# A transformer block of one core: order of every engine written by hand, attention in slices, opening tile by tile

## The chip, the cores and the metric

The kernel runs on one core of a Trainium2 chip. The metric is the time of one execution on the device in microseconds (us). "Span" is the time from the first to the last instruction of the one execution that was profiled; it is about 1.8 us shorter than the time that the same execution is given (842.8 against 844.55 us before). A run counts as slow when it takes over 1.5% more than the fastest run of its kernel; all timed runs below were in the fast state. The one exception is a single look whose state is not known, and it is named as such. In the views of the profile PE is TensorE, PEld its weight loads, DVE VectorE, ACT ScalarE, POOL GpSimd and SP SyncE; L12 is line 12 of that kernel's code.

## The reference, cut to what matters

One block: layernorm, a QKV projection, a sliding dilated attention (each position looks at 8 keys, two positions apart), an output projection with residual, a second layernorm, and a feed-forward part in which a gate product and an up product are multiplied and projected down.

```python
def _A_ref(x, wqkv, wo):                       # x: 1 x 2048 x 1024, 32 heads of 32
    q, k, v = split_heads(x @ wqkv)
    idx = pos[:, None] - 2 * arange(8)[None, :]          # 8 keys, dilation 2
    logits = einsum("bhsd,bhswd->bhsw", q, k[idx]) * scale      # masked where idx < 0
    o = einsum("bhsw,bhswd->bhsd", softmax(logits), v[idx])
    return merge_heads(o) @ wo
# ... (cut)
h  = x + _A_ref(layernorm(x), wqkv, wo)
n  = layernorm(h)
h2 = h + ((n @ w_gate) * (n @ w_up)) @ w_down            # 1024 -> 3584 -> 1024
```

## The kernel before

The 2048 positions are done in four chunks of 512. The matmuls run on TensorE and write to tiles in PSUM; such a tile can be filled anew when another engine has read it (`PE ps <- ACT sg` in the views below is a wait for that). The attention of a chunk has no matmul: VectorE does it as products, sums and a softmax over tiles of 128 partitions (4 parts of the chunk x 32 heads), which takes about 84 us a chunk. It needs a layout other than the one that the projections give, so ScalarE copies each QKV result out of PSUM, SyncE stores it to DRAM (`qd`, `kd`, `vd`), and GpSimd loads it back in the attention's layout (`qD`, `kD`, `vD`). The keys and values of a part include a halo, the positions just before it, which its first queries look at. The attention's result `oD` goes to DRAM and comes back transposed as `oT`, the operand of the output projection.

The order of instructions is left to the framework's scheduler, steered by priorities (`prio`); a low priority makes attention fill the gaps of everything else. Projections and feed-forward use six PSUM tiles, transposes two more.

```python
    psmm = ctx.enter_context(tc.tile_pool(name="psmm", bufs=6, space=PSUM))
    pstp = ctx.enter_context(tc.tile_pool(name="pstp", bufs=2, space=PSUM))
# ... (cut)
    def attention(c):
        qD = att.tile([128, DH, SUB], BF, tag="qD")
        kD = att.tile([128, DH, SUB + HB], BF, tag="kD")
        vD = att.tile([128, DH, SUB + HB], BF, tag="vD")
        nc.gpsimd.dma_start(qD[:], qd[c].rearrange("c g d s -> (c g) d s"))
        # ... (cut: halo copies DRAM to DRAM, loads of kD and vD, all on GpSimd)
        for wp in range(W // 2):
            prod = att.tile([128, 2, DH, SUB], BF, tag="prod")
            for j in range(2):
                o = HB - DIL * (2 * wp + j)
                nc.vector.tensor_tensor(prod[:, j], qD[:], kD[:, :, o:o + SUB], ALU.mult)
            # ... (cut: sums over DH, softmax, products with vD, sums into oD)
        nc.gpsimd.dma_start(od[c].rearrange("c g d s -> (c g) d s"), oD[:])
        for cp in range(4):
            nc.gpsimd.dma_start(oT[:, :, cp, :], od[c][cp].rearrange("(hg hl) d s -> (hl d) hg s", hl=4))
        return oT

    def wo_ln2(c, oT):
        # ... (cut: loads of four x tiles into hs, of the weights)
        for hf in range(2):
            for t in range(4):
                ps = psmm.tile([128, 512], F32, tag="mm")
                # ... (cut: 8 matmuls of oT and wo)
                nc.vector.tensor_tensor(hs[t][:, bass.ts(hf, 512)], ps[:], hs[t][:, bass.ts(hf, 512)], ALU.add)
        for t in range(4):
            layernorm_T(hs[t], lnT, t * 128)
        return lnT, hs
# ... (cut)
    for c in range(NCH):
        qkv(c, lnTs[c], B0)                       # blocks 0 to 2 of 6
        if c + 1 < NCH:
            with prio(-10000 + 1000 * (c + 1)):
                lnTs[c + 1] = ln1(c + 1)
        else:
            with prio(1000000):
                oT = attention(0)
            nxt = wo_ln2(0, oT)                   # between the halves of the last QKV
        qkv(c, lnTs[c], B1)
    for c in range(NCH):
        lnT2, hs = nxt
        hT = ffn1(c, lnT2)                        # gate/up
        if c + 1 < NCH:
            with prio(1000000 + (c + 1) * 20000):
                oT = attention(c + 1)
            nxt = wo_ln2(c + 1, oT)
        ffn2(c, hT, hs)                           # down
```

Of the kernel before, what the change touches and what calls it, by code (L numbers as in the profile page):

```python
# [16 lines left out]
D = 1024  # L17
H = 32
DH = 32
# [3 lines left out]
HALO = (W - 1) * DIL  # L23
# [7 lines left out]
NEG = -1.0e9  # L31




@with_exitstack
def kernel(
# [18 lines left out]
    @contextmanager  # L56
    def prio(base):
        with tc.high_priority(offset=tc.cur_priority - base):
            yield

    const = ctx.enter_context(tc.tile_pool(name="const", bufs=1))
    wpool = ctx.enter_context(tc.tile_pool(name="wstream", bufs=6))
    lnTp = ctx.enter_context(tc.tile_pool(name="lnT", bufs=3))
    lnp = ctx.enter_context(tc.tile_pool(name="ln", bufs=4))
    xp = ctx.enter_context(tc.tile_pool(name="xp", bufs=4))
# [4 lines left out]
    psmm = ctx.enter_context(tc.tile_pool(name="psmm", bufs=6, space=PSUM))  # L70
    pstp = ctx.enter_context(tc.tile_pool(name="pstp", bufs=2, space=PSUM))
    dram = ctx.enter_context(tc.tile_pool(name="dram", bufs=1, space=DRAM))

    nc.scalar.preload_act_table_set("natural_log_exp_and_others")
    ident = const.tile([128, 128], BF)
    make_identity(nc, ident[:])
    eps = const.tile([128, 1], F32)
    nc.vector.memset(eps[:], EPS)
    mask = const.tile([32, W, 16], F32)
    nc.vector.memset(mask[:], 0.0)  # L80
    for w in range(1, W):
        nc.vector.memset(mask[:, w, 0:DIL * w], NEG)
    zt = const.tile([32, DH, HB], BF)
    nc.vector.memset(zt[:], 0.0)
# [12 lines left out]
    def layernorm_T(src, dstT, col, xbar=True):  # L97
        st = small.tile([128, 2, nc.vector.BN_STATS_DIM], F32, tag="st")
        for i in range(2):
            nc.vector.bn_stats(out=st[:, i, :], in_=src[:, bass.ts(i, 512)])  # L100
        mv = small.tile([128, nc.vector.BN_AGGR_DIM], F32, tag="mv")
        nc.vector.bn_aggr(out=mv[:], in_=st[:])  # L102
        lnv = small.tile([128, 1], F32, tag="lnv")
        nc.scalar.activation(lnv[:], mv[:, 1:2], ACTF.Ln, bias=eps[:])  # L104
        rstd = small.tile([128, 1], F32, tag="rstd")
        nc.scalar.activation(rstd[:], lnv[:], ACTF.Exp, scale=-0.5)
        ln = lnp.tile([128, D], BF, tag="ln")
        nc.vector.tensor_scalar(ln[:], src[:], mv[:, 0:1], rstd[:], ALU.subtract, ALU.mult)
        if xbar:
            nc.sync.dma_start_transpose(dstT[:, :, col:col + 128], ln[:])  # L110
            return
        pt = pstp.tile([128, KO, 128], BF, tag="pt")
        for kk in range(KO):
            nc.tensor.transpose(pt[:, kk, :], ln[:, bass.ts(kk, 128)], ident[:])
        nc.scalar.copy(dstT[:, :, col:col + 128], pt[:])

    def ln1(c):
        lnT = lnTp.tile([128, KO, TC], BF, tag="lnT")
        for t in range(4):
            xt = xp.tile([128, D], BF, tag="x")  # L120
            nc.sync.dma_start(xt[:], x[bass.ds(c * TC + t * 128, 128), :])
            layernorm_T(xt, lnT, t * 128, xbar=(c > 0))
        return lnT

    wq_sb = []

    def qkv(c, lnT, blocks):
        for b in blocks:
            wt = wq_sb[b]
            pss = {}  # L130
            if c == 0 and b == 0:
                for j in range(4):
                    pss[j] = psmm.tile([128, TC], F32, tag="mm", name=f"ps0_{j}")
                for hf in range(2):
                    for j in range(4):
                        for ko in range(KO):
                            nc.tensor.matmul(pss[j][:, bass.ts(hf, 256)], lhsT=wt[:, ko, bass.ts(j, 128)],
                                             rhs=lnT[:, ko, bass.ts(hf, 256)],
                                             start=(ko == 0), stop=(ko == KO - 1))
            for j in range(4):  # L140
                m = b * 4 + j
                if j in pss:
                    ps = pss[j]
                else:
                    ps = psmm.tile([128, TC], F32, tag="mm")
                    for ko in range(KO):
                        nc.tensor.matmul(ps[:], lhsT=wt[:, ko, bass.ts(j, 128)], rhs=lnT[:, ko, :],  # L147
                                         start=(ko == 0), stop=(ko == KO - 1))
                sg = t1k.tile([128, TC], BF, tag="t1k")
                nc.scalar.copy(sg[:], ps[:])  # L150
                hg = m % 8
                if m < 8:
                    nc.sync.dma_start(qd[c][:, 4 * hg:4 * hg + 4, :, :].rearrange("c g d s -> (g d) c s"),
                                      sg[:].rearrange("p (c s) -> p c s", c=4))
                else:
                    dst = (kd, vd)[m // 8 - 1][c]
                    nc.sync.dma_start(dst[0, 4 * hg:4 * hg + 4, :, HB:HB + SUB].rearrange("g d s -> (g d) s"),
                                      sg[:, 0:SUB])
                    base = sg[:, SUB - HB:SUB - HB + 1]
                    win = bass.AP(base.tensor, base.offset, [list(base.ap[0]), [SUB, 3], [1, SUB + HB]])  # L160
                    nc.sync.dma_start(dst[1:4, 4 * hg:4 * hg + 4, :, :].rearrange("c g d s -> (g d) c s"), win)

    def attention(c):
        qD = att.tile([128, DH, SUB], BF, tag="qD")
        kD = att.tile([128, DH, SUB + HB], BF, tag="kD")
        vD = att.tile([128, DH, SUB + HB], BF, tag="vD")
        nc.gpsimd.dma_start(qD[:], qd[c].rearrange("c g d s -> (c g) d s"))
        for (tD, td) in ((kD, kd), (vD, vd)):
            if c == 0:
                nc.gpsimd.dma_start(td[c][0, :, :, 0:HB], zt[:])  # L170
            else:
                nc.gpsimd.dma_start(td[c][0, :, :, 0:HB], td[c - 1][3, :, :, SUB:SUB + HB])
            nc.gpsimd.dma_start(tD[:], td[c].rearrange("c g d s -> (c g) d s"))
        lg = att.tile([128, W, SUB], F32, tag="lg")
        for wp in range(W // 2):
            prod = att.tile([128, 2, DH, SUB], BF, tag="prod")
            for j in range(2):
                w = 2 * wp + j
                o = HB - DIL * w
                nc.vector.tensor_tensor(prod[:, j], qD[:], kD[:, :, o:o + SUB], ALU.mult)  # L180
            nc.vector.tensor_tensor(prod[:, :, 0:16], prod[:, :, 0:16], prod[:, :, 16:32], ALU.add)  # L181
            nc.vector.tensor_tensor(prod[:, :, 0:8], prod[:, :, 0:8], prod[:, :, 8:16], ALU.add)  # L182
            t3 = att.tile([128, 2, 4, SUB], F32, tag="t3")
            nc.vector.tensor_tensor(t3[:], prod[:, :, 0:4], prod[:, :, 4:8], ALU.add)  # L184
            nc.vector.tensor_tensor(t3[:, :, 0:2], t3[:, :, 0:2], t3[:, :, 2:4], ALU.add)
            nc.vector.tensor_tensor(lg[:, 2 * wp:2 * wp + 2, :], t3[:, :, 0], t3[:, :, 1], ALU.add)
        if c == 0:
            nc.vector.tensor_tensor(lg[0:32, :, 0:16], lg[0:32, :, 0:16], mask[:], ALU.add)
        tr = att.tile([128, 4, SUB], F32, tag="t3")
        nc.vector.tensor_tensor(tr[:], lg[:, 0:4], lg[:, 4:8], ALU.max)  # L190
        nc.vector.tensor_tensor(tr[:, 0:2], tr[:, 0:2], tr[:, 2:4], ALU.max)
        mx = att.tile([128, SUB], F32, tag="mx")
# [3 lines left out]
        tr2 = att.tile([128, 4, SUB], F32, tag="t3")  # L196
        nc.vector.tensor_tensor(tr2[:], lg[:, 0:4], lg[:, 4:8], ALU.add)
        nc.vector.tensor_tensor(tr2[:, 0:2], tr2[:, 0:2], tr2[:, 2:4], ALU.add)
        sm = att.tile([128, SUB], F32, tag="mx")
        nc.vector.tensor_tensor(sm[:], tr2[:, 0], tr2[:, 1], ALU.add)  # L200
        rs = att.tile([128, SUB], F32, tag="rs")
        nc.vector.reciprocal(rs[:], sm[:])
        at = att.tile([128, W, SUB], BF, tag="at")
        nc.vector.tensor_tensor(at[:], lg[:], rs[:, None, :].to_broadcast((128, W, SUB)), ALU.mult)
        oD = att.tile([128, DH, SUB], BF, tag="oD")
        for wp in range(W // 2):
            pv = att.tile([128, 2, DH, SUB], BF, tag="prod")
            for j in range(2):
                w = 2 * wp + j
                o = HB - DIL * w  # L210
                nc.vector.tensor_tensor(pv[:, j], vD[:, :, o:o + SUB],  # L211
                                        at[:, w, None, :].to_broadcast((128, DH, SUB)), ALU.mult)
            if wp == 0:
                nc.vector.tensor_tensor(oD[:], pv[:, 0], pv[:, 1], ALU.add)
            else:
                nc.vector.tensor_tensor(pv[:, 0], pv[:, 0], pv[:, 1], ALU.add)  # L216
                nc.vector.tensor_tensor(oD[:], oD[:], pv[:, 0], ALU.add)  # L217
        nc.gpsimd.dma_start(od[c].rearrange("c g d s -> (c g) d s"), oD[:])
        oT = att.tile([128, KO, 4, SUB], BF, tag="oT")
        for cp in range(4):  # L220
            nc.gpsimd.dma_start(oT[:, :, cp, :], od[c][cp].rearrange("(hg hl) d s -> (hl d) hg s", hl=4))
        return oT

    def wo_ln2(c, oT):
        lnT = lnTp.tile([128, KO, TC], BF, tag="lnT")
        hs = []
        for t in range(4):
            ht = hp.tile([128, D], BF, tag="h")
            nc.sync.dma_start(ht[:], x[bass.ds(c * TC + t * 128, 128), :])
            hs.append(ht)  # L230
# [125 lines left out]
```

## Time and profile before

| | before |
|---|---|
| time, median of 3 runs | 845.12 us (843.84 to 847.0) |
| span of the profiled run | 842.8 us |
| TensorE busy | 811.4 us, 96% of the span |
| VectorE busy | 464.9 us, 55% |
| one group of eight 512-column matmuls at full clock | 1.7265 us |
| 464 groups' worth of matmuls (the whole kernel) | 801 us |

TensorE bounds the kernel, and only about 42 us of the span are not matmuls at full rate. The question is always where those are. From the profile's page, the busy times and the granted TensorE clock (one digit for each fortieth of the span):

```profile
span 842.8 us, 9480 instructions
PE 811.4 (96%) x3702; PEld 372.0 (44%) x3776; DVE 464.9 (55%) x523; ACT 208.0 (25%) x393; POOL 30.1 (4%) x46
...
PEclk9999999989999998999999999999999999999999
```

The lower digits stand where TensorE has waited. The view of waits says for what (columns: engine, what it was to do, what released it, microseconds in total, times, longest):

```profile
PE pt L114 <- DVE ln L108: 6.9, 2, 6.6
PE ps L237 <- DMA oT<-od: 6.1, 1, 6.1
PE ps L147 <- ACT sg L150: 3.2, 1, 3.2
PE acc L293 <- DVE ht L239: 3.0, 3, 1.4
```

Four places: the opening (first layernorm), the wait for `oT` at the first projection, ScalarE held by the attention's exponential, and residual adds that free PSUM late at the second projection.

What matters later is VectorE at the end of the first attention. The timeline (columns: start, duration, engine, line, operation, how many; in brackets the idle time before and what ended it):

```profile
153.11 2.29 DVE L217 TENSOR_TENSOR oD<-oD,pv 128x4096 bf16<-128x4096 bf16 x1
155.44 4.50 DVE L180 TENSOR_TENSOR prod<-qD,kD 128x4096 bf16<-128x4096 bf16 x2
...
177.93 1.28 DVE L239 TENSOR_TENSOR ht<-ps,ht 128x512 bf16<-128x512 f32 x2
```

The last sum into `oD` ends at 155.4, and the next chunk's first product starts at once: its operands are there. The DMA queue of GpSimd shows why, in the same view:

```profile
107.34 0.55 POOL L167 DMA_DIRECT2D qD<-qd  x1 [6.00 <-DVE prod L180]
108.02 0.54 POOL L173 DMA_DIRECT2D kD<-kd  x1
...
155.70 0.55 POOL L218 DMA_DIRECT2D od<-oD  x1 [4.10 <-DMA wt<-in_A_wo_dram]
...
164.67 3.54 POOL L221 DMA_DIRECT2D oT<-od  x4 [7.65 <-DMA od<-oD]
```

The scheduler issued the next `qD` and `kD` at 107 us, 48 us ahead, as soon as the running attention had read its own for the last time. TensorE around it, from the projection to the first gate/up matmul:

```profile
170.64 4.88 PE L237 MATMUL ps<-wt,oT 128*128 128x512 bf16 x11 [6.12 <-DMA oT<-od]
...
207.94 1.89 PE L254 MATMUL pg<-lnT,wg 128*128 128x512 bf16 x7
```

So gate/up of chunk 0 starts at 207.9 us.

### The profile page before, as it was taken

The numbers are of one execution on the slowest core, as the hardware profiler recorded it, in microseconds if no ns is written. First come the engines' busy times: TensorE is split into PE (matmuls) and PEld (weight loads), VectorE is DVE, ScalarE is ACT, GpSimd is POOL, SyncE is SP. The second block draws the span as 40 slices with busy tenths as digits, with TensorE's granted clock in tenths as the row PEclk, the third lists the DMA queues.
The fourth block names the chain that finished last, engine by engine and source line by source line (L and its number), as shares of the span: only waits on it lengthen the run. The fifth ranks groups of instructions, "written<-read, shape, count | busy, mean of one in ns | idle before, by whom it ended". The sixth has DMA issues, their size and how long they took to land.

```text
span 842.8 us, 9480 instructions
## 1 busy us (share of the span) xinstructions
PE 811.4 (96%) x3702; PEld 372.0 (44%) x3776; DVE 464.9 (55%) x523; ACT 208.0 (25%) x393; POOL 30.1 (4%) x46
## 2 busy tenths in 40 slices
PE   5999989889999998999999999999999999999998
PEld 4444434334444443444444444444444444444443
DVE  6335999999999999999992421111116101111010
ACT  4443323203333320003333100133331003333100
POOL 1001000200001000010000010000000000000000
PEclk9999999989999998999999999999999999999999
DMA  9998983969949574886546498563537655454520
GB/s 271 261 227 192 234 239 87 278 160 243 288 162 290 161 267 102 289 243 201 165 135 219 150 178 263 189 197 103 198 97 210 185 186 174 135 165 130 174 71 25
DMA packets 196365, 158.97 MB, mean 189 GB/s; under 512 B 84576, under 2 KB 189024, under 8 KB 194272
## 3 DMA queue, kind: packets, MB, share of 16 engines
q1 hardware_dynamic: 192480, 136.08, 56.5%
q0 software_dynamic: 3840, 22.28, 8.3%
q8 instruction: 29, 0.48, 0.2%
q14 instruction: 16, 0.13, 0.1%
HBM read 129.17 MB, written 22.02 MB: 179 GB/s over the span
## 4 chain that ended last, share of the span: by engine, by line
PE 57%; DVE 15%; issue 4%; DMA 0%; ACT 0%; DVEq 0%; ACTq 0%
PE pg L254 17%; PE pu L258 17%; PE acc L293 17%; DVE pv L211 3%; PE ps L237 3%; PE accl L280 3%; DVE prod L180 2%; DVE pv L216 1%; DVE gs L264 1%; DVE oD L217 1%; DVE prod L181 1%; DVE t L184 1%; DVE prod L182 1%; DVE ht L239 1%; DMA vd<-sg 0%
## 5 line engine op out<-in xcount | busy, mean ns | idle before, releaser
L254 PE MATMUL pg<-lnT,wg 128*128 128x512 bf16 x879 | 210.1, 379 | 1.0
L258 PE MATMUL pu<-lnT,wu 128*128 128x512 bf16 x877 | 209.9, 379 | 0.9
L293 PE MATMUL acc<-wd,gs 128*128 128x512 bf16 x768 | 172.6, 383 | 5.2 <-DVE ht L239 3.0
L147 PE MATMUL ps<-lnT,wq 128*128 128x512 bf16 x722 | 160.1, 382 | 4.0 <-ACT sg L150 3.2
L264 DVE TENSOR_TENSOR gs<-gs,us 128x512 bf16<-128x512 bf16 x112 | 47.1, 422 | 193.3 <-ACT us L263 193.3
L254 PEld LDWEIGHTS <-wg 128*128 128x128 bf16 x896 | 87.7, 98 | 105.7
L258 PEld LDWEIGHTS <-wu 128*128 128x128 bf16 x896 | 87.6, 98 | 105.7
L261 ACT CAST gs<-pg 128x512 bf16<-128x512 f32 x112 | 65.6, 585 | 257.8 <-PE pg L254 252.1
L293 PEld LDWEIGHTS <-gs 128*128 128x128 bf16 x784 | 77.3, 99 | 99.9 <-issue 9.5
L147 PEld LDWEIGHTS <-wq 128*128 128x128 bf16 x736 | 72.5, 98 | 91.2 <-issue 5.7
L263 ACT CAST us<-pu 128x512 bf16<-128x512 f32 x112 | 65.6, 585 | 121.1 <-PE pu L258 113.0
L180 DVE TENSOR_TENSOR prod<-qD,kD 128x4096 bf16<-128x4096 bf16 x32 | 72.9, 2284 | 16.8 <-DMA kD<-kd 16.8
L296 DVE TENSOR_TENSOR ht<-acc,ht 128x512 bf16<-128x512 f32 x28 | 17.4, 683 | 106.0 <-PE acc L293 106.0
L150 ACT CAST sg<-ps 128x512 bf16<-128x512 f32 x96 | 54.9, 586 | 78.6 <-PE ps L147 69.2
L211 DVE TENSOR_TENSOR pv<-vD,at 128x4096 bf16<-128x4096 bf16 x32 | 72.4, 2287 | 0.3
L237 PE MATMUL ps<-wt,oT 128*128 128x512 bf16 x250 | 58.4, 391 | 7.8 <-DMA oT<-od 6.1
L237 PEld LDWEIGHTS <-oT 128*128 128x128 bf16 x256 | 25.7, 101 | 40.0 <-DMA oT<-od 6.6
L181 DVE TENSOR_TENSOR prod<-prod 128x4096 bf16<-128x4096 bf16 x16 | 36.6, 2287 | 0.4
L104 ACT ACTIVATE lnv<-mv,eps 128x1 f32<-128x1 f32 x32 | 9.3, 294 | 99.8 <-DVE mv L102 99.8
L100 DVE BATCH_NORM_STATS2 st<-xt 128x6 f32<-128x512 bf16 x32 | 20.3, 667 | 19.5 <-DMA xt<-in_A_x_dram 19.5
L216 DVE TENSOR_TENSOR pv<-pv 128x4096 bf16<-128x4096 bf16 x12 | 27.4, 2287 | 0.2
L217 DVE TENSOR_TENSOR oD<-oD,pv 128x4096 bf16<-128x4096 bf16 x12 | 27.4, 2285 | 0.2
(50 smaller groups left out, 265.9 us busy)
## 6 DMA issues: line engine op xcount, KB each, us to landing
wg<-in_B_w_gate_dram SPq DMA_DIRECT2D x28, 1024.0 KB, 5.4
wu<-in_B_w_up_dram SPq DMA_DIRECT2D x28, 1024.0 KB, 6.7
wd<-in_B_w_down_dram SPq DMA_DIRECT2D x32, 896.0 KB, 5.3
wt<-in_A_wo_dram SPq DMA_DIRECT2D x8, 1024.0 KB, 7.1
wq<-in_A_wqkv_dram SPq DMA_DIRECT2D x6, 1024.0 KB, 7.2
kD<-kd POOLq DMA_DIRECT2D x4, 1152.0 KB, 8.4
vD<-vd POOLq DMA_DIRECT2D x4, 1152.0 KB, 7.5
xt<-in_A_x_dram SPq DMA_DIRECT2D x16, 256.0 KB, 4.6
```

Source lines behind the costliest of these rows:

```text
L147: nc.tensor.matmul(ps[:], lhsT=wt[:, ko, bass.ts(j, 128)], rhs=lnT[:, ko, :], start=(ko == 0), stop=(ko == KO - 1))
L150: nc.scalar.copy(sg[:], ps[:])
L180: nc.vector.tensor_tensor(prod[:, j], qD[:], kD[:, :, o:o + SUB], ALU.mult)
L181: nc.vector.tensor_tensor(prod[:, :, 0:16], prod[:, :, 0:16], prod[:, :, 16:32], ALU.add)
L211: nc.vector.tensor_tensor(pv[:, j], vD[:, :, o:o + SUB], at[:, w, None, :].to_broadcast((128, DH, SUB)), ALU.mult)
L237: nc.tensor.matmul(ps[:], lhsT=oT[:, kk, t, :], rhs=wt[:, kk, :], start=(kk == 0), stop=(kk == KO - 1))
L254: nc.tensor.matmul(pg[:], lhsT=wg[:, ko, bass.ts(j, 128)], rhs=lnT[:, ko, :], start=(ko == 0), stop=(ko == KO - 1))
L258: nc.tensor.matmul(pu[:], lhsT=wu[:, ko, bass.ts(j, 128)], rhs=lnT[:, ko, :], start=(ko == 0), stop=(ko == KO - 1))
L261: nc.scalar.copy(gs[:], pg[:])
L263: nc.scalar.copy(us[:], pu[:])
L264: nc.vector.tensor_tensor(gs[:], gs[:], us[:], ALU.mult)
L293: nc.tensor.matmul(acc[t][:], lhsT=hT[f][:, bass.ts(t, 128)], rhs=wd[:, j, :], start=(f == 0), stop=(f == NF - 1))
```

## The change

The intent: the scheduler is switched off (`manual_schedule`) and every engine's order is the order of the code. A small pacing class holds generators; after each matmul group the code calls `bg.step(1.73)`, which emits as much background work (slices of attention, layernorms) as fits a credit of estimated microseconds. Other parts: one pool of eight PSUM tiles in place of six and two; weights through a ring of seven tiles; the opening done row tile by row tile, after 13 dummy matmuls that are to bring TensorE's clock up; the halo of keys and values stored straight from SBUF in place of DRAM-to-DRAM copies.

```diff
-    psmm = ctx.enter_context(tc.tile_pool(name="psmm", bufs=6, space=PSUM))
-    pstp = ctx.enter_context(tc.tile_pool(name="pstp", bufs=2, space=PSUM))
+    psum = ctx.enter_context(tc.tile_pool(name="psum", bufs=8, space=PSUM))
+    ctx.enter_context(tc.manual_schedule())
 ... (cut)
+    for i in range(13):
+        nc.tensor.matmul(wps[:], lhsT=warm[:, 0:128], rhs=warm[:], start=True, stop=True)
 ... (cut)
+    def first_tile(t):
+        stats(x0[t], mv0, t)
+        rstd_of(mv0, rs0, t, t + 1)
+        ln = normalize(x0[t], mv0, rs0, t)
+        pt = psum.tile([128, KO, 128], BF, tag="mm", name=f"pt{t}")
+        for kk in range(KO):
+            nc.tensor.transpose(pt[:, kk, :], ln[:, bass.ts(kk, 128)], ident[:])
+        nc.vector.tensor_copy(lnTs[0][:, 0:4, bass.ts(t, 128)], pt[:, 0:4, :])
+        nc.scalar.copy(lnTs[0][:, 4:8, bass.ts(t, 128)], pt[:, 4:8, :])
 ... (cut)
     def attention(c):
 ... (cut: tiles)
+        nc.gpsimd.dma_start(qD[:], qd[c].rearrange("c g d s -> (c g) d s"))
+        nc.gpsimd.dma_start(kD[:], kd[c].rearrange("c g d s -> (c g) d s"))
+        nc.gpsimd.dma_start(vD[:], vd[c].rearrange("c g d s -> (c g) d s"))
+        yield 0.1
 ... (cut)
+                nc.vector.tensor_tensor(prod[:, j], qD[:], kD[:, :, o:o + SUB], ALU.mult)
+                yield 2.3
 ... (cut: the same operations as before, each followed by a yield of its estimated time)
+        nc.gpsimd.dma_start(od[c].rearrange("c g d s -> (c g) d s"), oD[:])
+        for cp in range(4):
+            nc.gpsimd.dma_start(oT[:, :, cp, :], od[c][cp].rearrange("(hg hl) d s -> (hl d) hg s", hl=4))
 ... (cut)
+                nc.vector.tensor_tensor(hs[t][:, bass.ts(hf, 512)], ps[:], hs[t][:, bass.ts(hf, 512)], ALU.add)
+                bg.spend(0.7)
+                bg.step(GROUP_US)
+            retire()
+        rest = norm_rest(hs, lnT, mv4, rs4)
+        bg.add(rest, first=True)
 ... (cut)
+    qkv(0, range(1, 6))
+    start_attention(0)
+    bg.add(ln1(3), first=True)
+    qkv(1, range(6))
+    start_attention(1)
+    qkv(2, range(6))
+    start_attention(2)
+    qkv(3, range(4), last=True)
+    bg.finish(atts[0])
+    bg.rate = 0.85
+    nxt = wo_ln2(0)
+    qkv(3, range(4, 6), last=True)
+    start_attention(3)
```

The three loads are the first lines of the attention's generator, and attention c+1 is not begun before attention c has emitted its last line, the four loads of `oT`. On GpSimd's queue the next chunk's loads therefore stand behind the store of `oD` and the loads of `oT`.

## The prediction

> What bounds it now. The page gives TensorE 96% busy of an 842.8 us span. In the timeline a group of eight 512-column matmuls takes 1.7265 us; 464 groups' worth of work is 801 us. The other 42 us, read from the same timeline:
> - opening: the first full group starts at 21.4 us, with 6.9 us of useful work before it: 14.5 us;
> - 21 to 208 us (QKV and the first output projection): 13.9 us. Stalls 3.2 us (ScalarE, held 11.3 us by the softmax exponential, keeps six PSUM tiles) and 6.1 us (oT transfer); the rest is half clock after each (windows: granted clock 0.5 to 0.6 for 4 to 5 us). The Trainium skill ("TensorE: Matmul & The Clock Gate", Part 1) says an idle window sends the clock to half; this trace agrees;
> - 305 to 376 us: 9.3 us, PSUM held until VectorE, busy with attention, does the residual adds;
> - tail 3.9 us. From 376 to 839 us nothing is lost.
>
> What the change does. Same arithmetic. Eight PSUM tiles shared instead of six should remove the 3.2 us stall. Small halo copies replace DRAM-to-DRAM ones. Opening: 13 dummy matmuls, then stats, normalise, transposes, copies tile by tile. On VectorE each tile now waits for the previous tile's PSUM copy: about 0.5 + 1.4 + 0.8 + 0.6 + 0.8 us. With tile 0 normalised near 6.1 us, tile 3 lands near 19 us; the 256-column matmuls take 3.5 us warm or 7 cold. So the first full group starts near 23 us: no gain, about 2 us lost. Pre-warming is spent before these waits.
>
> The order listing shows what I think costs most. The GpSimd queue is fixed: store oD, four oT loads, and only then the next chunk's qD, kD, vD loads. Before, they were issued early (next qD at 107 us, used at 155 us). From the trace: store to oT issue 9 us, oT issues 3.5 us, kD landing 8.4 us: VectorE idles about 21 us after each attention. And its next chunk's first slices (17 us of products and sums, at 2.29 and 1.23 us) stand ahead of the projection's residual adds, which free PSUM.
>
> With B the start of the first full group: attention 0 starts near B+50 (after chunk 3's layernorm) and takes 84 us as before (71.6 to 155.4): T = B+134. oT lands at T+15, TensorE arrives at B+145: a 4 us stall. Projection groups fill all eight PSUM tiles by T+32; the first add comes at T+39: 7 us. Adds end T+50, layernorm and transposes T+64, while only eight QKV groups cover it: about 9 us more. The gate/up matmuls start near B+198 = 221 us, against 208 before: +13.
>
> The next boundary: attention 1 ends about 17 us before gate/up 0 does, and the 21 us hole plus 14 us of slices delays the adds; about 11 us lost (9.3 before). The third: about 4 us (0 before). The last: 0.
>
> Sum: 801 + 16 (opening) + 26 (first boundary) + 11 + 4 + 4 = 862 us span, 2.3 more as timed. I temper this: an author who paced it by measured durations probably looked at traces. Prediction 860, range 838 to 878; faster 0.09, same 0.45, slower 0.46.
>
> Right if: VectorE shows idle holes near 20 us released by qD/kD transfers after each of the first three attentions; TensorE waits on residual adds at the first two projections; gate/up 0 starts after 215 us; no stall near the exponential of attention 0; first full group at 21 to 26 us.
>
> Wrong if: qD/kD land much sooner; x loads of chunk 3 come earlier, so attention 0 starts before B+45; the pre-warmed opening reaches B below 20; or the opposite, ScalarE held by a late layernorm statistic in chunk 3, which would add a stall.

## The result, and the profile after

| | before | after |
|---|---|---|
| time, median of 4 runs each, same rounds | 845.36 us | 891.79 us (882.21 to 894.87) |
| ratio, 95% interval | | 1.053 (1.0445 to 1.0614) |
| span of the profiled run | 842.8 us | 888.4 us |
| TensorE clock granted, mean | 0.989 | 0.967 |
| VectorE busy | 464.9 us | 467.9 us |
| weight loads busy (PEld) | 372.0 us | 372.7 us |

A ratio here is the mean time of one kernel's fast runs over that of the other's of the same rounds, so it is not quite the ratio of the medians quoted beside it. The changed kernel is 5% slower. The prediction had the holes and put its odds on slower by a hair (0.46 against 0.45 for the same), but 860 with a top of 878 was too low.

The work is the same (VectorE and weight loads differ by less than 1%); TensorE waits more. The page:

```profile
span 888.4 us, 9700 instructions
PE 822.9 (93%) x3821; PEld 372.7 (42%) x3821; DVE 467.9 (53%) x520; ACT 198.0 (22%) x351; POOL 51.3 (6%) x96
...
PEclk9999999986799999899999979999999999999999
```

The clock has a trough in the ninth to eleventh slice (178 to 244 us), and two more at 355 to 377 and 511 to 533 us. What TensorE waited for:

```profile
PE acc L440 <- DVE h L391: 18.2, 4, 6.9
PE ps L296 <- DVE h L391: 15.3, 1, 15.3
PE pg L296 <- DMA lnT<-ln: 9.2, 1, 9.2
PE wo L389 <- DMA oT<-od: 7.5, 3, 6.3
PE pt L269 <- DVE ln L170: 3.9, 3, 3.1
PE ps L296 <- ACT sg L242: 2.7, 1, 2.7
```

The first two lines, 33.5 us, name the residual adds of the projections (`h`), which free PSUM. The adds are short; what kept them? VectorE at the end of the first attention:

```profile
164.78 2.29 DVE L372 TENSOR_TENSOR oD<-oD,pv 128x4096 bf16<-128x4096 bf16 x1
193.66 4.49 DVE L324 TENSOR_TENSOR prod<-qD,kD 128x4096 bf16<-128x4096 bf16 x2 [26.58 <-DMA kD<-kd]
...
210.83 1.28 DVE L391 TENSOR_TENSOR h<-wo,h 128x512 bf16<-128x512 f32 x2
```

Where before the next product followed at once, VectorE now stands still for 26.58 us until `kD` lands. Then come 17 us of the next chunk's products and sums, which stand ahead of the adds in its queue, and the first add starts at 210.8. The Trainium skill ("TensorE: Matmul & The Clock Gate", Part 1, on engine queue depths) calls VectorE's queue strict FIFO; the trace agrees: the adds' PSUM was full from about 196 us on, and none went ahead of the products. One operand of the adds came late, too. The projection's x rows were issued on SyncE only with the projection:

```profile
176.98 4.71 SPq L182 DMA_DIRECT2D h<-in_A_x_dram  x4
```

They took 18.2 to 20.2 us to land, so by about 197 to 199 us. The adds could not have begun before that, and the products held them for some 12 to 14 us beyond it, not for all of the 15.3 us that TensorE waited.

The same hole comes after each of the first three attentions; in the groups of instructions (after the bars: busy time and mean nanoseconds, then the idle time before and its releaser):

```profile
L324 DVE TENSOR_TENSOR prod<-qD,kD 128x4096 bf16<-128x4096 bf16 x32 | 72.4, 2284 | 75.1 <-DMA kD<-kd 75.1
```

GpSimd's queue, to compare with the one before:

```profile
167.37 0.54 POOL L374 DMA_DIRECT2D od<-oD  x1 [20.72 <-DVE oD L372]
174.86 3.55 POOL L377 DMA_DIRECT2D oT<-od  x4 [6.95 <-DMA od<-oD]
178.40 0.56 POOL L315 DMA_DIRECT2D qD<-qd  x1
178.95 0.55 POOL L316 DMA_DIRECT2D kD<-kd  x1
```

The load of `kD` is issued at 178.95, after the round trip of `oD`, and lands 14.6 us later (12.2 median over the four chunks, 8.4 before). And TensorE:

```profile
179.06 3.59 PE L389 MATMUL wo<-w_wo,oT 128*128 128x512 bf16 x8 [6.28 <-DMA oT<-od]
...
211.57 16.56 PE L296 MATMUL ps<-lnT,w_qkv 128*128 128x512 bf16 x64 [15.29 <-DVE h L391]
237.31 3.56 PE L296 MATMUL pg<-lnT,w_wg 128*128 128x512 bf16 x8 [9.19 <-DMA lnT<-ln]
```

Eight matmuls take 3.6 us right after such a wait; at full clock the same view gives 1.89 (1.73 from one start to the next). The windows view gives a granted clock of 0.53 at 178 to 183 and at 237 to 241 us. This is called half clock below. Gate/up of chunk 0 starts at 237.3, 70.2 us after the attention's end.

The span can now be summed for both kernels. Each boundary is the time between two starts read in the timeline, less the groups of matmuls between them at 1.7265 us (the first: from the first full group to gate/up 0, less 100 groups, 172.65 us). The opening is the start of the first full group less the 6.9 us of matmul work done by then; the tail is what follows the last matmul:

| us | before | predicted | after |
|---|---|---|---|
| all matmuls at full clock (464 x 1.7265) | 801.1 | 801 | 801.1 |
| opening | 14.5 | 16 | 17.8 |
| first boundary (QKV, first projection, to gate/up 0) | 13.9 | 26 | 40.0 |
| half clock at the start of gate/up 0 | 0 | 0 | 1.7 |
| second boundary | 9.3 | 11 | 12.2 |
| third boundary | 0 | 4 | 11.8 |
| tail | 3.9 | 4 | 3.8 |
| sum | 842.7 | 862 | 888.4 |

### The profile page after: what moved, and what is told of

It is laid out like the page before. It is cut to its first block, busy times and chain, and to the rows that moved or that the text cites. A ratio compares the mean times of both kernels' runs of the same rounds, so it can differ in the third digit from the quotient of the medians.

```text
span 888.4 us, 9700 instructions
## 1 busy us (share of the span) xinstructions
PE 822.9 (93%) x3821; PEld 372.7 (42%) x3821; DVE 467.9 (53%) x520; ACT 198.0 (22%) x351; POOL 51.3 (6%) x96
## 4 chain that ended last, share of the span: by engine, by line
PE 67%; DVE 10%; DMA 6%; issue 1%; SPq 1%; POOL 0%; ACT 0%; POOLq 0%; DVEq 0%; ACTq 0%
PE pg L296 19%; PE acc L440 19%; PE pu L296 19%; PE ps L296 5%; DVE prod L324 4%; DMA kD<-kd 3%; PE accl L430 3%; PE wo L389 2%; DVE prod L326 1%; DMA od<-oD 1%; DVE t L331 1%; SPq L182 1%; DVE prod L328 1%; DVE h L391 1%; DMA h<-in_A_x_dram 1%
## 5 line engine op out<-in xcount | busy, mean ns | idle before, releaser
L296 PE MATMUL pg<-lnT,w_wg 128*128 128x512 bf16 x896 | 213.3, 381 | 9.2 <-DMA lnT<-ln 9.2
L296 PE MATMUL pu<-lnT,w_wu 128*128 128x512 bf16 x896 | 211.7, 379 | 0.0
L440 PE MATMUL acc<-w_wd,gs 128*128 128x512 bf16 x784 | 174.4, 384 | 18.3 <-DVE h L391 18.2
L296 PE MATMUL ps<-lnT,w_qkv 128*128 128x512 bf16 x736 | 161.9, 383 | 18.0 <-DVE h L391 15.3
L296 PEld LDWEIGHTS <-w_wg 128*128 128x128 bf16 x896 | 87.9, 98 | 116.1 <-issue 11.3
L296 PEld LDWEIGHTS <-w_wu 128*128 128x128 bf16 x896 | 87.8, 98 | 106.0 <-issue 0.6
L296 PEld LDWEIGHTS <-w_qkv 128*128 128x128 bf16 x736 | 72.7, 99 | 106.9 <-issue 22.0
L324 DVE TENSOR_TENSOR prod<-qD,kD 128x4096 bf16<-128x4096 bf16 x32 | 72.4, 2284 | 75.1 <-DMA kD<-kd 75.1
L389 PE MATMUL wo<-w_wo,oT 128*128 128x512 bf16 x256 | 58.3, 387 | 8.0 <-DMA oT<-od 7.5
L420 DVE TENSOR_TENSOR h<-acc,h 128x512 bf16<-128x512 f32 x28 | 17.4, 682 | 63.4 <-PE acc L440 63.4
L161 DVE BATCH_NORM_STATS2 st<-x 128x6 f32<-128x512 bf16 x32 | 20.0, 668 | 40.1 <-DMA x<-in_A_x_dram 40.1
## 6 DMA issues: line engine op xcount, KB each, us to landing
kD<-kd POOLq DMA_DIRECT2D x4, 1152.0 KB, 12.2
```

Of the source, the lines that this page charges most:

```text
L296: nc.tensor.matmul(ps[:], lhsT=wt[:, ko, bass.ts(j, 128)], rhs=rhs[:, ko, :], start=(ko == 0), stop=(ko == KO - 1))
L389: nc.tensor.matmul(ps[:], lhsT=oTs[c][:, kk, t, :], rhs=wt[:, kk, :], start=(kk == 0), stop=(kk == KO - 1))
L440: nc.tensor.matmul(acc[t][:], lhsT=hT[f][:, bass.ts(t, 128)], rhs=wts["wd", c, hf, b][:, j, :], start=(f == 0), stop=(f == NF - 1))
```

## The experiments

**Theory A**: the loads behind the attention's round trip make the holes; the holes hold up the residual adds, and these hold PSUM and TensorE. **Rival B**: the attention simply ends too late (at 167.1 us against 155.4), because the opening is slower and chunk 3's x tiles come late. **Rival C**: slices placed ahead of the adds are enough by themselves, hole or not. And a side question, what the dummy matmuls do. The kernel before was timed anew beside each batch of runs; its medians were 846.44 us (e1 to e4), 845.43 (e5 to e8) and 846.8 (f1 and f2).

In what follows T is the end of attention 0 and F0 the start of gate/up 0.

### e1_prefetch: the next chunk's loads early

```diff
+    def load_qk(c):
+        qD = att.tile(...); kD = att.tile(...)
+        nc.gpsimd.dma_start(qD[:], ...); nc.gpsimd.dma_start(kD[:], ...)
+        qk[c] = (qD, kD)
 ... (in attention, behind the last of the four product loops)
+        if c + 1 in stored:
+            load_qk(c + 1)
```

> Only the place of the next chunk's qD and kD loads on the GpSimd queue changes: right after the last product of the running attention instead of behind its store and the four oT loads. Theory A (the 22 to 27 us VectorE holes, with slices queued ahead of the residual adds, are most of the loss): no hole over 3 us; from the end of attention 0 to the first gate/up matmul about 48 us instead of 70; the second and third boundary lose at most 3 us each instead of 12; span about 846 us. Rival B (attention 0 starting at 83 us, because chunk 3's x loads wait in the SyncE queue, is most of the loss and the holes are slack): the span falls by less than 12 us, to 876 or more.

Measured: 848.13 us, ratio 1.0024 (1.0009 to 1.0039), span 845.8. VectorE's line at the end of attention 0 (T = 167.91), in the timeline of this kernel:

```profile
167.94 4.50 DVE L332 TENSOR_TENSOR prod<-qD,kD 128x4096 bf16<-128x4096 bf16 x2
```

No idle time is noted: the hole is gone. TensorE in the same kernel:

```profile
179.85 16.34 PE L399 MATMUL wo<-w_wo,oT 128*128 128x512 bf16 x64 [6.24 <-DMA oT<-od]
196.03 13.98 PE L296 MATMUL ps<-lnT,w_qkv 128*128 128x512 bf16 x64
218.76 3.26 PE L296 MATMUL pg<-lnT,w_wg 128*128 128x512 bf16 x8 [8.75 <-DMA lnT<-ln]
```

The wait for the adds (15.29 us) is gone too, although the same products and sums (17 us of them) still stand ahead of the adds. VectorE is done with these early and even waits for the projection's x rows:

```profile
192.19 1.37 DVE L401 TENSOR_TENSOR h<-wo,h 128x512 bf16<-128x512 f32 x2 [6.99 <-DMA h<-in_A_x_dram]
```

So the slices alone, without the hole, cost nothing: rival C, which said "hole or not", falls. F0 is T + 50.9, close to before's T + 52.5; from F0 to the end TensorE takes 627.0 us against 651.1 in the changed kernel, so the second and third boundaries lose nothing (the 1.6 us left before gate/up 1 are the half clock at F0). The place of two loads in one queue is worth 42.6 us of the 45.6 us between the spans of the changed kernel and the kernel before, though attention still ends at 167.9. Theory A holds; B as the main cause falls.

### e2_hold: the holes stay, but no slice ahead of the adds

```diff
+        while c > 0 and c not in opened:      # first line after the loads in attention
+            yield "later", 0.5
 ... (opened.add(c + 1) when the layernorm behind projection c is emitted)
```

> Loads stay late, so the holes stay, but no slice of the next attention is put before the residual adds and the layernorm of the boundary. Theory A says a hole alone is harmless there, and costs only through the slices queued ahead of the adds: from the end of attention 0 to the first gate/up matmul 46 to 50 us, with no wait of QKV matmuls on residual adds, although a VectorE hole before the first slice remains. The price comes a stage later: attention 1 starts its slices about 40 us after attention 0's end, ends when gate/up 0 ends or after, and its oT is then up to 15 us late. Span 860 to 885. If instead the hole itself is the cost, this stage stays near 70 us. Rival B: no change in this stage beyond a few us.

Measured: 871.05 us, ratio 1.0291 (1.0266 to 1.0317), span 869.8. VectorE at the end of attention 0 (T = 168.42):

```profile
166.13 2.29 DVE L375 TENSOR_TENSOR oD<-oD,pv 128x4096 bf16<-128x4096 bf16 x1
196.80 5.12 DVE L394 TENSOR_TENSOR h<-wo,h 128x512 bf16<-128x512 f32 x8 [28.39 <-DMA h<-in_A_x_dram]
...
209.98 4.48 DVE L327 TENSOR_TENSOR prod<-qD,kD 128x4096 bf16<-128x4096 bf16 x2
```

VectorE still idles, now waiting for the projection's own x rows, but the adds come first, and F0 is T + 53.1. 2.5 us of waiting for adds remain, and F0 is a little later than the expected T + 46 to 50. So at the first boundary the hole costs only because slices stand ahead of the adds; with e1, where the slices cost nothing without the hole, it takes both together. The price is paid later. Attention 1 starts 42 us after attention 0 has ended, and the second projection waits for it:

```profile
PE wo L392 <- DMA oT<-od: 22.5, 2, 18.5
```

The idle time of VectorE therefore has to go, not merely be moved; keeping the slices back is not the cure. From the second boundary on this run tells nothing about holes, for the edit does more than its heading says: while attention 1 is held, the pacer already begins attention 2, so the `kD` loads of chunks 2 and 3 (issued at 266.8 and 411.3 us) stand ahead of the store of the `oD` before them, as in e1, and VectorE waits for no `kD`.

### e3_x3early: chunk 3's x tiles loaded earlier

```diff
-    bg.add(ln1(2))
+    late3 = ln1(3)
+    def ln1_2_then_x3():
+        yield from ln1(2)
+        next(late3)                # issues the x loads of chunk 3
+    bg.add(ln1_2_then_x3())
 ...
-    bg.add(ln1(3), first=True)
+    bg.add(late3, first=True)
```

> Chunk 3's x loads move ahead of most vd stores of chunk 0 on the SyncE queue. Attention 0 then starts near 72 us instead of 83, ends near 156, and the 2.7 us TensorE stall at its exponential goes. Theory A: everything to the first gate/up matmul moves by about 11 us and nothing more: span 875 to 880. Rival B: 20 us or more, span below 868.

Measured: 879.8 us, ratio 1.0396 (1.0354 to 1.0438), span 873.8. Attention 0 starts at 71.3 in place of 82.9 and T is 155.48, as in the kernel before, and the exponential stalls nothing. Yet the hole is still there and the adds still hold TensorE, for 16.4 us at the first boundary and for 14.5 us at the later ones (a line of the timeline, then one of the view of waits):

```profile
176.08 4.50 DVE L330 TENSOR_TENSOR prod<-qD,kD 128x4096 bf16<-128x4096 bf16 x2 [20.60 <-DMA kD<-kd]
...
PE ps L302 <- DVE h L397: 16.4, 1, 16.4
```

B is real, with 14.6 us between the profiled spans (12.0 between the medians, of different rounds), but it is not the main part of the loss.

### e4_open: statistics of the next tile ahead of the copy of the last

```diff
-    first_tile(0)
-    first_mm(ps0, 0, 0, 128)
-    first_tile(1)
 ...
+    first_norm(0)                  # stats, rstd, normalise
+    first_norm(1)
+    first_turn(0)                  # transposes and copies
+    first_mm(ps0, 0, 0, 128)
+    first_norm(2)
+    first_turn(1)
 ...
```

> Only the opening changes: on VectorE the next tile's statistics and normalise come before the copy of the tile before. The first full QKV group starts near 20 us instead of 24.7, with the last 256-column matmuls at full rate. If the rest simply follows, the span falls by 4 to 5 us, to about 884; if attention 0's start is bound by the x loads of chunk 3 rather than by the opening, it falls less, by 2 us or so.

Measured: 885.09 us, ratio 1.0461 (1.0444 to 1.0477), span 882.4. The first full group starts at 21.81 us in place of 24.67, later than the expected 20. Attention 0 starts at 82.3 all the same, for VectorE waits 25.95 us for chunk 3's x tiles. For this case 2 us or so were expected; the span fell by 6.0, which is not resolved: one execution of the changed kernel (882.21 us) was faster than all four of e4 (883.93 to 886.02), and the first hole was 21.1 us here against 26.6, with the same loads in the same order.

### e7_nowarm: one dummy matmul instead of 13

```diff
-    for i in range(13):
+    for i in range(1):
```

> The change as given with 1 dummy matmul instead of 13. The opening's waits are VectorE's chain of statistics, normalise and copies, and in the changed kernel the last 256-column matmuls ran at half rate anyway after a 3.1 us wait. So the first full group starts within 2 us of the changed kernel's 24.7 us (24.5 to 26.2 seen in the runs so far): the dummies buy nothing that lasts. If pre-warming matters, it starts at 27 us or later.

Measured in one look, whose state is not known: 887.74 us, span 886.0. The opening of the changed kernel, and then of this one (the view ends at 30 us, so the last line of each is not the whole stretch):

```profile
9.71 1.74 PE L276 MATMUL ps<-lnT,w_qkv 128*128 128x128 bf16 x28 [1.49 <-DMA w_qkv<-in_A_wqkv_dram]
...
20.17 4.66 PE L276 MATMUL ps<-lnT,w_qkv 128*128 128x256 bf16 x32 [0.51 <-DVE lnT L270]
24.67 5.56 PE L296 MATMUL ps<-lnT,w_qkv 128*128 128x512 bf16 x25
```

```profile
9.61 3.17 PE L276 MATMUL ps<-lnT,w_qkv 128*128 128x128 bf16 x28 [0.94 <-DMA w_qkv<-in_A_wqkv_dram]
...
21.95 6.13 PE L276 MATMUL ps<-lnT,w_qkv 128*128 128x256 bf16 x32 [0.51 <-DVE lnT L270]
27.92 2.32 PE L296 MATMUL ps<-lnT,w_qkv 128*128 128x512 bf16 x10
```

With the dummies the first full group starts 3.25 us earlier than without: the first 28 matmuls run at full in place of nearly half rate (1.74 against 3.17 us), and the last 32 lose less (4.66 against 6.13 us). In e1, e2 and e3, whose openings are that of the changed kernel, it starts at 25.96, 26.23 and 24.47, so the one execution without the dummies is 1.7 to 3.5 us later. The expectation (within 2 us, or 27 us and later if pre-warming matters) and "Pre-warming is spent before these waits" were too strong. Nothing of it shows in the whole: one execution of each cannot tell 886.0 from 888.4 when the runs of the changed kernel lie 13 us apart.

### e8_before_psum8: the kernel before with one pool of eight PSUM tiles

```diff
-    psmm = ... bufs=6
-    pstp = ... bufs=2
+    psmm = ... bufs=8
 ... (transposes take their tile from psmm too)
```

> The kernel before with the change's one shared pool of eight PSUM tiles instead of six plus two for transposes, nothing else. ScalarE is held 11.3 us by the exponential of attention 0; eight tiles cover 13.8 us of matmul groups, six only 10.4. The 3.2 us TensorE stall and the 1.7 us at half clock after it go: 840 to 842 us by time, 0.4 to 0.6% faster. Rival: the oT wait that follows grows by as much, and nothing changes.

Measured: 842.39 us, ratio 0.9971 (0.9945 to 0.9998), span 841.3. The stall at the exponential falls from 3.23 to 1.73 us, where it was expected to go, and the wait for `oT` that follows grows from 6.12 to 7.43: most of what is won in front of a fixed wait is waited out there. The opening, in which the transposes now share the pool, is 1.3 us longer.

### e5_all: e1, e3 and e4 together

> The three mends together: early qD and kD loads, early x loads of chunk 3, reordered opening. If their gains add where they act (F0 is the start of gate/up 0): first full group near 21.8 us, attention 0 ends near 155.5 us, oT lands before TensorE needs it, gate/up 0 starts about 50 us later, near 203 to 207 us (before 208, e1 219), nothing lost after; span 829 to 834 us, 1 to 1.7% faster than before. If the gains overlap (one hides the other), span 838 or more.

Measured: 844.05 us, ratio 0.9972 (0.9953 to 0.999), span 842.2. The gains did not add up: the branch "overlap" of the expectation came true. T is 159.66, 8.3 us earlier than in e1, but F0 (213.94) only 4.8 us earlier. In place of the removed waits came a stall of 4.6 us at the exponential (2.3 in e1), 1.9 us for adds whose x rows land late, and 10.9 us in front of gate/up 0 (8.8 in e1).

### e6_lnpipe: layernorm of each row tile right behind its adds

The two loops of the projection are swapped (row tile outside, half inside), and tiles 0 to 2 are normalised and transposed as soon as both their halves are added; tile 3 is left to the pacer.

```diff
-        for hf in range(2):
-            for t in range(4):
+        for t in range(4):
+            for hf in range(2):
 ... (matmuls and add as they were)
+                if hf == 1 and t < 3:
+                    for _ in tile_ln(t):
+                        bg.spend(_)
 ...
-        rest = norm_rest(hs, lnT, mv4, rs4)
+        rest = tile_ln(3)
         bg.add(rest, first=True)
```

> e5 with the output projection's loops swapped, so that each 128-row tile of the residual is complete after two groups and its layernorm and transpose follow at once, instead of all four after the eighth. The roughly 9 us that gate/up 0 waits for the last transpose should fall to 3 to 5 us: span 824 to 829, 4 us under e5. If VectorE, with 23 us of slices ahead of the adds, sets the pace instead, the gain is under 2 us.

Measured: 842.47 us, ratio 0.9977 (0.9959 to 0.9995), span 837.2. A miss: the wait in front of gate/up 0 shrank to 7.2 us only, and the gain over e5 is not resolved (the medians differ by 1.6 us, the runs of e6 lie 7 us apart, and the profiled one is the fastest of them). VectorE's and ScalarE's part was done at 199 us; SyncE's queue, in the timeline, shows what held the last transpose:

```profile
187.71 8.79 SPq L414 DMA_TRANSPOSE lnT<-ln  x3
...
197.91 1.46 SPq L250 DMA_DIRECT2D vd<-sg  x1
...
205.79 1.24 SPq L414 DMA_TRANSPOSE lnT<-ln  x1
```

The transpose was issued at 205.8, behind stores of values, because the pacer emitted it after them.

### f1_lnfirst: x rows early, last tile not left to the pacer

```diff
-        hs = load_x(c, "h")
+        hs = h0 if c == 0 else load_x(c, "h")      # h0 loaded before the last chunk's QKV
 ...
-                if hf == 1 and t < 3:
+                if hf == 1:
 ...
-        rest = tile_ln(3)
-        bg.add(rest, first=True)
+        rest = None
```

> The version with the layernorm per row tile (span 837.2) with two more changes: the x rows for the first projection's residual adds are loaded before the last chunk's QKV groups instead of at the projection, and the last row tile's layernorm is emitted right behind its add, ahead of the QKV groups that follow. In that version's trace the last normalise was done at 199.0 us but its transpose was issued by SyncE at 205.8, behind value stores, and gate/up 0 started at 209.5 after a 7.2 us wait; VectorE waited 2.3 us for the x rows. If emission order on those queues is what is left: the 7.2 us wait goes, gate/up 0 starts at 201 to 204 us, span 829 to 832, ratio to before 0.983 to 0.989. If the transfers themselves are slow (landing delayed by other traffic, not by order): the wait stays over 4 us and the span stays over 834.

Measured: 829.04 us (827.03 to 831.96, 5 runs), ratio 0.9803 (0.9781 to 0.9826), span 825.3, clock 0.998. TensorE at the first boundary:

```profile
172.25 13.99 PE L427 MATMUL wo<-w_wo,oT 128*128 128x512 bf16 x64 [3.35 <-DMA oT<-od]
186.07 13.98 PE L310 MATMUL ps<-lnT,w_qkv 128*128 128x512 bf16 x64
199.88 1.89 PE L310 MATMUL pg<-lnT,w_wg 128*128 128x512 bf16 x8
```

From the projection to gate/up 0 nothing is waited for; F0 falls by 9.6 us to 199.9, and the span by 11.9. The profiled execution is the fastest of five (the other spans are 826.5 to 830.2), so most of them beat the expected 829 to 832, partly because the projection and gate/up 0 no longer start at half clock (1.7 us each in e6). This version beats both kernels: 2.0% below before in the same rounds, though its interval reaches across 2%.

### f2_split5: one more QKV block ahead of the projection

```diff
+        if c == 0:
+            yield 10.0                             # ahead of the exponential
 ...
-    qkv(3, range(4), last=True)
+    qkv(3, range(5), last=True)
```

> The former, with the first attention's exponential emitted about six groups later (it held ScalarE 14 us before) and one more block of four QKV groups moved ahead of the first projection, so that they fill the wait for the attention output. Expected: no stall at the exponential, attention 0 ends at 157 to 160 us as before, the projection starts at once or with under 2 us of wait at about 173, gate/up 0 starts at 194 to 198, span 822 to 827, ratio to before 0.975 to 0.981. If the layernorm chain after the projection takes longer than four groups (6.9 us), the wait for the last transpose comes back at 3 us or more and the span is 828 or more.

Measured: 834.75 us, ratio 0.9863 (0.9845 to 0.9881), span 832.7. The expectation's second branch came true, and the kernel is slower than f1. As intended, the exponential and the first `oT` stall nothing, but only four groups now cover the layernorm chain: TensorE waits 3.6 us, starts gate/up 0 at half clock, and F0 is 198.3, only 1.5 us earlier. From F0 to gate/up 1 it then takes 166.5 us against 158.9 in f1: the second projection waits 3.2 us for its `oT` (which f1 has in time) and 1.8 us on adds, and starts at half clock again. Two edits were made at once, and no run separates them.

## Why the prediction was right or wrong

**Right.** The direction, by a hair (0.46 against 0.45, and 860 is itself only 1.7% above before); the mechanism read from the order of GpSimd's queue ("store oD, four oT loads, and only then the next chunk's qD, kD, vD loads"), which e1 shows by undoing it; holes near 20 us released by `kD` after the first three attentions (26.6, 22.4 and 26.1); TensorE waiting for residual adds; gate/up 0 after 215 us; the second boundary (12.2 against 11), the opening to within 2 us, no loss at the last.

**Wrong in size.** The sum was 862, the span 888.4. Of the 26.4 us between them 14.0 lie at the first boundary (26 predicted, 40.0 lost), 7.8 at the third, and the rest is small. The steps that failed:

1. "Attention 0 starts near B+50 [...]: T = B+134." It was B + 142.4 (B = 24.67, T = 167.1). The x tiles of chunk 3 were issued on SyncE only at 71.9 us, behind stores of values, and VectorE idled 26.3 us for them. Under "wrong if" the text named an earlier start, and a late statistic of chunk 3 only as something that holds ScalarE; that hold came (10.1 us) and stalled nothing, while the lateness of the attention cost time. e3 measures the term. There T is B + 131.0, and the first boundary loses 27.5 us, near the predicted 26 (T falls by 11.6 us and the span by 14.6). Part of this is a hole that was shorter as well (point 2): with the late start and a hole of 21.1 us, e4 and e7 lose 36.8 and 33.7 us at this boundary, so the late start alone is worth some 6 to 9 us of it, an estimate from these single executions. ScalarE, held 14.35 us by the exponential, also stalled TensorE for 2.7 us where none was predicted. That the late start did this is not shown: e3, which starts attention early, has no such stall (held 8.1 us), but e5, which starts it early too, has 4.6 (held 16.2).
2. "kD landing 8.4 us" was taken from a trace in which GpSimd issued the load with `qD` alone before it. Issued behind four `oT` loads and together with `qD`, `vD`, x rows and weights it took 14.6 us here; in the windows view the DMA engines are busy throughout (share 1.06 at 183 to 188 us) with 357 GB/s. (Before they were busy too when `kD` loaded, 1.06 and 320 GB/s at 108 to 118 us; what differs is what was issued beside it. No run isolates this.) The Trainium skill ("Trainium Kernel Development and Optimization", Key Constraints) says that DMAs of all issuing queues share the same 16 engines and interleave; this trace agrees: from 179 to 194 us GpSimd's queue took 70.4% of the 16 engines' time and the hardware queue, with x rows and weights, 28.7%. The hole became 26.6 instead of 21 us, the first add came at T + 43.8 instead of T + 39, and F0 at T + 70.2 instead of B + 198, which is T + 64. The size of 21 was nevertheless not bad, with some luck: e3, e4 and e7 load in the same order, and their first holes were 20.6, 21.1 and 21.1 us, because `kD` took longer than predicted (11.0 to 11.4 us) and the time from the store of `oD` to the first `oT` load was shorter (5.2 to 5.5 us instead of 9). And `oT` let the projection start at T + 12.0 instead of T + 15, so PSUM was full at T + 29.2 instead of T + 32: the wait for the adds was 15.3 us where 7 were predicted, 4.8 of it from the later first add and 2.8 from the earlier full PSUM.
3. "The third: about 4 us (0 before)." It was 11.8: the same hole (26.1 us) as at the second boundary delays the adds as much as there. The 4 had been a guess without a sum behind it; e1, which removes the hole, makes this loss zero.
4. "I temper this" took 4 us off the sum on the ground that the author probably looked at traces. Nothing in the profile supported that, and the range's top of 878 left only 14 us for errors that mostly had the same sign: a later start delays a hole, and a longer hole delays adds.

The terms do not simply add up: e1 alone removes 42.6 us of span, e3 alone 14.6 and e4 alone 6.0 (the last not resolved), 63 in all, of a difference of 45.6.

**Half clock.** The Trainium skill ("TensorE: Matmul & The Clock Gate", Part 1) gives half rate after an idle window of about 3.4 us, and a start-to-start time of 215.7 ns for warm 512-column matmuls. The trace agrees with the second (1.7265 us / 8 = 215.8 ns), and with the first in kind: waits of 6.28, 15.29 and 9.19 us were followed by a granted clock of 0.50 to 0.53 in the windows view. Taking what is left of the loss as its cost, it took 5.3 us at the first boundary (40.0 less the waits of 2.7 + 7.5 + 15.3 + 9.2) against 4.6 before (13.9 less 3.2 + 6.1), so it does not explain the miss.

**Open.** The runs of the changed kernel spread over 12.7 us (before: 3.2), and only one of them has a trace. The holes hint at transfers: the first was 26.6 us in that trace and 21.1 us in e4 and e7, which differ from it only in the opening; that this makes the spread is not shown. In f1 two changes were made at once, so the 11.9 us are not split between them.

## What to carry to other kernels

When a scheduler is replaced by a hand-written order, list for every DMA queue what each prefetch now stands behind; a load that moves behind a round trip of the data of its predecessor turns into a hole of the round trip plus a landing time under load. On an in-order engine, work that frees a resource of the bottleneck (here adds that free PSUM, and the transpose that starts the next matmuls) is best emitted ahead of work that only fills time (the slices cost nothing in e1, where they were over in time, but 15.3 us of TensorE behind a hole); a pacer that spreads by estimated durations does not know the difference. The same hand-written order beat the scheduler by about 2% (1.7 to 2.2%) once these places were put right, and on the way the gains did not add: in e5 other waits took the place of part of those removed.

## What the Trainium skill lacked or had wrong

- "TensorE: Matmul & The Clock Gate", Part 1, ties half rate to an idle window of about 3.4 us; its passage on cycling through PSUM tells of short idles that bring it too, without a figure. Shorter gaps had it here: after one of 2.29 us in e4's opening 32 matmuls of 128 columns took 3.67 us, and in e1's opening 28 took 2.81 after gaps of 0.52 and 1.28 us with four matmuls between. But the length of the gap does not decide alone: in e5 the same gap of 2.29 us was followed by full rate (28 in 1.72 us), and so was 0.51 and 1.49 us in the changed kernel (28 in 1.74). The page calls the window free-running, so a gap may fall differently into it; no run here tests that.
- "DMA: Bandwidth & Descriptors" treats the order of completion, but I found no figure there for how much later a load lands when others are issued beside it: 1152 KB took 8.4 us (median of four) in the kernel before, where `vD` was not issued with it, and 12.2 us (median of four, up to 14.6) in the changed kernel, where `vD` was, and three of the four stood behind `oT` loads.
- "Perfetto Trace Analysis" (Optimization Strategy) says to find the gaps on the contended engine and what blocks it, and to make those dependencies start sooner or complete faster. The first step names the residual adds here (33.5 us), which take 0.7 us each and are innocent. The page could say plainly that the blocker's own queue has to be read in turn: the cause stood two steps back, in the wait of VectorE for `kD` (75.1 us) and in GpSimd's issue order.
- No page that I used gives a figure for what a transfer loses that stands behind others in an issuing queue: in e6 the last transpose was issued 6.8 us after its operand was done (199.0 to 205.8 us), and f1, which moved it ahead, took F0 down by 9.6 us together with the earlier x rows.
